# A fused attention and two-MLP kernel on one core: the last stage gets five pairs of operand buffers instead of four, and six output buffers instead of four

## The chip, the core and the metric

The kernel runs on one core of a Trainium2 chip. The metric is the device time of one launch in microseconds (us). TensorE is called PE, VectorE DVE, ScalarE ACT, GpSimd POOL; SP is the engine that here only issues transfers (its queue is "SPq" in the rows).

## What is computed

Three parts follow each other (attention, a gated MLP, a leaky MLP), all in float32:

```python
p_packed = sm_attn(p, k, v)            # softmax(p k' / 8) v, 8 batches, 8 heads, 576 x 64, 32 packs
out = sm_attn(q, p_packed, p_packed)
x = out.transpose(0, 2, 1, 3).reshape(4608, 512)
x2 = ((x @ w1) * (x @ w2)) @ w3 @ wo1          # 512 -> 1024 -> 1024 -> 512
h = x2 @ w_in                                  # 512 -> 2048
y = np.maximum(0.01 * h, h) @ w_out            # 2048 -> 512, the result
```

The change touches the last two lines, called the last stage here.

## The kernel before

**Precision.** Every operand of these products is split into a high and a low half that PE can multiply exactly enough, and each product is three matmuls (high by high, high by low, low by high). So operands come in pairs of tiles: `xh` and `xl` for x2, `gh` and `gl` for the activations.

**Last stage.** It multiplies in the manner of Strassen: seven products of sums of quarter matrices in place of eight products. The sums are called forms. The forms of x2 (seven for each group of 768 tokens, six groups) are made once, in high and low halves, by `stage`, and written to the DRAM tensor `xfd` (L557). The hidden width is cut into three parts F (3, 3 and 2 chains wide). For each F and each group, that is for 18 units `t`, `h_unit` reads the seven forms and makes h, `g_ops` makes the forms of the activations, and `o_unit` multiplies by the forms `wo` of the second weights. The product of one form of x2 takes 6 matmuls for each chain. `o_unit` adds to a running output: for F = 0 it starts it, for F = 1 and 2 `begin_o` loads the partial sums from the DRAM tensor `part` (L798), and L817 stores them to `part`, in F = 2 to `out`.

**Buffers.** `load_forms` takes a tile `xh` and a tile `xl` for each form from XF pairs of buffers and issues the two reads, 384 KB each (L660); a read can only be issued when PE has finished with the form that held the buffers before. The output tiles `o` come from OB buffers; a load at L798 into one has to wait until the store at L817 from the same buffer has landed in DRAM. All of these transfers (L557, L553, L650, L660, L687, L798, L817) stand in SP's one queue: while SP waits for one, all behind it wait too.

**Order.** The code is written unit by unit: reads of the first four forms of unit t+1, then `o_unit(t-1)` with its stores, then the reads of the other three. The order in which instructions stand on each engine is not that of the code: a scheduler lays them out by its own estimate of times, one list for each engine, and each engine works through its list in order.

**Memory.** The pool `b1` (forms of the weights `wi`, then `xr`, `xh`, `xl`, `xt`) grows from the left over what attention held; on the right the pool `wts` (converted weights `w`, and `ppT`) lies until the end of attention, and `b2` (`wo`, `gr`, `gs`, `gh`, `gl`, `o`) later takes the right side. Ahead of the last stage `make_wi(0)` builds the forms of the first weights (L535 sums, L539 casts, L135 subtractions) and `stage_b(2, 1)` makes a part of the x2 forms, both beside the last batch: its gated products `ab` (ACT copies `a` at L427, DVE multiplies at L433, ACT casts at L438, DVE subtracts at L135; PE's products at L130 go to PSUM in two tiles for each, four tiles in all) and `M` (PE at L163, ACT at L401, DVE at L135). Then PE makes x2 (L449, printed as L130) from the `ab` tiles, and after that begins the last stage at L746.

Of the kernel before, what the change touches and what calls it, by code (L numbers as in the profile page):

```python
# [55 lines left out]
def tile_kernel(ctx, tc, qT, kT, vL, pT, w12, w3b, wo1, win, wo2, out):  # L56
# [571 lines left out]
    PARTS = ((0, 3), (6, 3), (12, 2))  # L628
    TB = 3 * NB
    ORDER = (1, 2, 6, 5, 7, 4, 3)  # L630
    XF, XR, XT, GR, GS, GH, GL, OB = 4, 5, 2, 5, 2, 5, 5, 4
    wi = {m: b1.tile([P, 2, 2, 384], F32R, name=f"wi{m}") for m in ORDER}

    def form_w(w, size):
# [256 lines left out]
```

## Time and profile before

| | before |
|---|---|
| median of 3 runs | 1306.71 us (1303.98 to 1311.98) |
| the profiled execution | 1311.57 us, its span on the core 1309.8 us |
| PE matmuls busy | 1267.4 us, 97% of the span |
| PE weight loads busy | 1170.2 us, 89% |
| DVE busy | 871.9 us, 67% |
| ACT busy | 609.7 us, 47% |
| POOL busy | 102.3 us, 8% |
| chain that ended last | PE 86%, DMA 9%, DVE 2%, issue 2%, SP's queue 1% |
| mean rate of the transfers | 216 GB/s |

A busy time says how long an engine had work under way, and the chain follows from the end of the program back through whatever was waited for. The profiled execution is 4.86 us above the median and close to the slowest of the three runs.

### The profile page before, as it was taken

The page shows a single profiled execution, that of the slowest core. Times are in us where ns is not written, and L with a number is a line of the kernel's source. Part 1 is how long each engine was busy: PE and PEld are TensorE (multiplying, and loading weights), DVE is VectorE, ACT ScalarE, POOL GpSimd, SP SyncE. Part 2 cuts the span into 40 slices and gives each one's busy share as a digit, 9 for nine tenths or more (in the row PEclk, how much of TensorE's full clock was granted, in tenths as well). Part 3 has the DMA queues.
Part 4 walks back from the last instruction along what each step waited for, and adds up shares of the span by engine and source line. Part 5 has one row for each costly group of instructions (what it writes and reads, how often), then busy time and mean ns, then how long its engine had stood idle before and what let it go on. Part 6 is the DMA issues. An engine that isn't in the chain of part 4 may idle for free.

```text
span 1309.8 us, 23357 instructions
## 1 busy us (share of the span) xinstructions
PE 1267.4 (97%) x8984; PEld 1170.2 (89%) x8984; DVE 871.9 (67%) x1449; ACT 609.7 (47%) x1141; POOL 102.3 (8%) x87
## 2 busy tenths in 40 slices
PE   5999999999999999999999999989999999999898
PEld 1458998989898989899999999989999999899898
DVE  5897465776776769709865765677457549576667
ACT  3445344454545455526655546463334343443332
POOL 4543011111110100000000000000000000000000
PEclk8999999999999999999999999999999999999999
DMA  9944254666573836438789767383754583878874
GB/s 341 349 154 158 63 160 138 206 211 228 188 253 123 284 117 225 160 109 301 251 285 311 276 215 241 121 276 135 265 194 156 181 279 131 316 255 294 273 265 156
DMA packets 139375, 283.08 MB, mean 216 GB/s; under 512 B 14848, under 2 KB 66048, under 8 KB 139264
## 3 DMA queue, kind: packets, MB, share of 16 engines
q1 hardware_dynamic: 130048, 272.16, 60.9%
q10 hardware_dynamic: 9216, 9.44, 2.1%
q8 instruction: 70, 1.15, 0.4%
q14 instruction: 41, 0.34, 0.1%
HBM read 202.38 MB, written 79.17 MB: 215 GB/s over the span
## 4 chain that ended last, share of the span: by engine, by line
PE 86%; DMA 9%; DVE 2%; issue 2%; SPq 1%; ACT 0%; POOL 0%; POOLq 0%; ACTq 0%; DVEq 0%
PE mm L130 29%; PE b L746 27%; PE c L746 14%; PE a L746 7%; PE mm L379 4%; PE at L163 4%; DMA xh<-xfd 3%; DMA xl<-xfd 1%; PE at L221 1%; DMA wi<-wid 1%; DMA v<-vL 1%; DMA part<-o 1%; DMA xr<-x2d 1%; PE at L202 0%; DMA c<-w3b 0%
## 5 line engine op out<-in xcount | busy, mean ns | idle before, releaser
L130 PEld LDWEIGHTS mm<-AT,M 128*128 128x128 f32 x1536 | 208.4, 189 | 33.2 <-issue 9.7
L130 PE MATMUL mm<-AT,M 128*128 128x288 f32 x1536 | 223.9, 301 | 6.1 <-DVE M L135 2.7
L746 PE MATMUL b<-xh,wi 128*128 128x384 f32 x768 | 218.9, 337 | 9.2 <-DMA xh<-xfd 5.6
L746 PE MATMUL b<-gh,wo 128*128 128x384 f32 x768 | 213.9, 335 | 1.6 <-DVE o L709 1.4
L130 PEld LDWEIGHTS mm<-ab,W 128*128 128x128 f32 x1536 | 203.5, 188 | 8.3 <-ACT x2s L454 5.0
L130 PE MATMUL mm<-ab,W 128*128 128x288 f32 x1536 | 207.3, 295 | 0.0
L746 PEld LDWEIGHTS b<-xh,wi 128*128 128x128 f32 x768 | 141.5, 189 | 11.6 <-ACT gr L706 4.4
L746 PEld LDWEIGHTS b<-gh,wo 128*128 128x128 f32 x768 | 140.3, 188 | 2.5 <-issue 1.0
L746 PE MATMUL b<-xl,wi 128*128 128x384 f32 x384 | 129.3, 337 | 0.4 <-DMA xl<-xfd 0.4
L746 PE MATMUL b<-gl,wo 128*128 128x384 f32 x384 | 128.4, 334 | 0.0
L746 PE MATMUL c<-xh,wi 128*128 128x384 f32 x384 | 106.7, 337 | 4.1 <-DMA xh<-xfd 3.9
L746 PE MATMUL c<-gh,wo 128*128 128x384 f32 x384 | 107.2, 335 | 0.5 <-DVE o L704 0.5
L539 ACT CAST gh<-gr 128x1152 fp32r<-128x1152 f32 (+1 forms) x72 | 75.6, 1052 | 67.1 <-PE b L746 32.5
L135 DVE TENSOR_TENSOR gl<-gr,gh 128x1152 fp32r<-128x1152 f32 (+1 forms) x72 | 87.4, 1219 | 21.2 <-ACT gh L539 21.2
L433 DVE TENSOR_TENSOR ab<-mm,a 128x288 f32<-128x288 f32 x128 | 57.8, 453 | 54.4 <-PE mm L130 34.3
L539 ACT CAST gh<-gs 128x1152 fp32r<-128x1152 f32 (+1 forms) x54 | 56.9, 1054 | 61.6 <-PE b L746 32.4
L135 DVE TENSOR_TENSOR ab<-ab,ab 128x288 fp32r<-128x288 f32 x119 | 59.8, 506 | 33.7 <-ACT ab L438 32.1
L694 ACT ACTIVATE gr<-gr 128x1152 f32<-128x1152 f32 (+1 forms) x54 | 57.3, 1062 | 47.2 <-DVE gr L709 46.8
L379 PE MATMUL mm<-ab,w 128*128 128x512 f32 x128 | 61.6, 633 | 15.3 <-POOL ab L290 10.4
L438 ACT CAST ab<-ab 128x288 fp32r<-128x288 f32 x128 | 55.1, 432 | 45.3 <-DVE ab L433 45.0
L746 PEld LDWEIGHTS c<-xh,wi 128*128 128x128 f32 x384 | 69.8, 188 | 6.4 <-DMA xh<-xfd 5.6
L746 PEld LDWEIGHTS b<-xl,wi 128*128 128x128 f32 x384 | 72.5, 189 | 1.2 <-DMA xl<-xfd 1.2
(119 smaller groups left out, 2020.4 us busy)
## 6 DMA issues: line engine op xcount, KB each, us to landing
xh<-xfd SPq DMA_DIRECT2D x126, 384.0 KB, 5.6
xl<-xfd SPq DMA_DIRECT2D x126, 384.0 KB, 5.2
part<-o SPq DMA_DIRECT2D x48, 384.0 KB, 3.3
o<-part SPq DMA_DIRECT2D x48, 384.0 KB, 4.0
c<-wo SPq DMA_DIRECT2D x20, 512.0 KB, 5.1
xfd<-xt SPq DMA_DIRECT2D x49, 192.0 KB, 3.0
xfd<-xr SPq DMA_DIRECT2D x49, 192.0 KB, 3.4
raw<-kT SPq DMA_DIRECT2D x32, 288.0 KB, 5.4
```

What stands on the lines that cost most here:

```text
L130: ins = nc.tensor.matmul(dst, lhs(i), rhs(j), start=first and n == 0, stop=last and n == 2)
L135: engine.tensor_tensor(out=out, in0=x, in1=rd(hi), op=ALU.subtract)
L163: ins = nc.tensor.matmul(dst(h)[c * 32:c * 32 + 32], lhs[r, c, :], rhs(c)[r], start=True, stop=True)
L221: ins = nc.tensor.matmul(ps[r, :64], PT[:K, c, r], v[:K, c, g * 64:g * 64 + 64], start=c == 0, stop=c == 4)
L379: nc.tensor.matmul(w13p[fc], words["3", i][:, c:c + P], words["o", jc], start=w13n[fc] == 1, stop=w13n[fc] == 8)
L433: nc.vector.tensor_tensor(out=t, in0=pb[:, :TH], in1=a, op=ALU.mult)
L438: nc.scalar.copy(t[:, 0], ab32[fc, th])
L539: nc.scalar.copy(hi[step], x[step])
L694: nc.scalar.activation(out=out, in_=x, func=AF.Prelu, alpha=0.01)
L746: nc.tensor.matmul(dst, lhs(l), rhs(r), start=first and n == 0, stop=last and n == total - 1, skip_group_check=True)
```

## The change

```diff
-    XF, XR, XT, GR, GS, GH, GL, OB = 4, 5, 2, 5, 2, 5, 5, 4
+    XF, XR, XT, GR, GS, GH, GL, OB = 5, 5, 2, 5, 2, 5, 5, 6
```

XF goes from 4 to 5 pairs `xh`, `xl` and OB from 4 to 6 tiles `o`; each of the four added tiles takes 3,072 bytes of every partition. No arithmetic, no transfer and no byte is added or removed. Two things follow from it in the built program. Pool `b1` now ends at byte 86,144 of a partition instead of 79,984, and `wts` begins at 83,040, so that `b1` now reaches into the memory of `wts`: the last tiles `xt` and `xl` come to lie on `ppT` and `w`. And the scheduler lays out another order on all engines but POOL.

The first place is SP's queue at the step from F = 0 to F = 1 (`o_9927` to `o_9930` are the outputs of the last unit of F = 0, `o_10407` and on those of the next units, `wo...` the new second weights, `xh_9880`, `xh_9884` forms of the first unit of F = 1). Before:

```order
L687 DMA wo7_7437<-wod_62 128x3x256
L817 DMA part_7440<-o_9929 128x768
L798 DMA o_10409<-part_7440 128x768
L798 DMA o_10411<-part_7440 128x768
L687 DMA wo4_7438<-wod_62 128x3x256
L817 DMA part_7440<-o_9930 128x768
L660 DMA xl_9881<-xfd_81 128x768
L660 DMA xh_9880<-xfd_81 128x768
```

After:

```order
L687 DMA wo7_7437<-wod_62 128x3x256
L817 DMA part_7440<-o_9927 128x768
L798 DMA o_10411<-part_7440 128x768
L817 DMA part_7440<-o_9928 128x768
L687 DMA wo4_7438<-wod_62 128x3x256
L817 DMA part_7440<-o_9930 128x768
L817 DMA part_7440<-o_9929 128x768
L798 DMA o_10413<-part_7440 128x768
```

The load of `wo4` stood behind two loads of `o`; now it stands behind one, and ahead of it there are only a load of `o` and two stores.

The second place is SP's queue in F = 2 (`o_13339` and its like are outputs, `xh_13582` and `xh_13586` the next forms). Before:

```order
L660 DMA xh_13470<-xfd_81 128x768
L817 DMA out<-o_13339 128x768
L798 DMA o_13629<-part_7440 128x768
L660 DMA xl_13583<-xfd_81 128x768
L660 DMA xh_13582<-xfd_81 128x768
L817 DMA out<-o_13341 128x768
L817 DMA out<-o_13343 128x768
L817 DMA out<-o_13345 128x768
L798 DMA o_13631<-part_7440 128x768
L660 DMA xl_13587<-xfd_81 128x768
L660 DMA xh_13586<-xfd_81 128x768
```

After:

```order
L660 DMA xh_13470<-xfd_81 128x768
L817 DMA out<-o_13339 128x768
L660 DMA xl_13583<-xfd_81 128x768
L660 DMA xh_13582<-xfd_81 128x768
L798 DMA o_13633<-part_7440 128x768
L660 DMA xl_13587<-xfd_81 128x768
L660 DMA xh_13586<-xfd_81 128x768
L817 DMA out<-o_13343 128x768
L660 DMA xl_13591<-xfd_81 128x768
L817 DMA out<-o_13341 128x768
```

The reads of `xl_13587` and `xh_13586` stood behind three stores and a load of `o`, and now stand ahead of these three stores; the load of `o` in front of them is another one.

The third place is DVE ahead of the last stage, at the last gated products of the last batch (`ab32_7114` is the fifth of seven after `M_6921`). Before:

```order
L135 TENSOR_TENSOR M_6921<-at_6912,M_6921 128x1024
L433 TENSOR_TENSOR ab32_6952<-mm_6937,a_6950 128x288
L135 TENSOR_TENSOR xr_7201<-xr_7201,xt_7392 128x384
L433 TENSOR_TENSOR ab32_7025<-mm_7010,a_7023 128x288
L135 TENSOR_TENSOR ab_6954<-ab32_6952,ab_6954 128x288
L433 TENSOR_TENSOR ab32_7062<-mm_7047,a_7060 128x288
L135 TENSOR_TENSOR ab_7027<-ab32_7025,ab_7027 128x288
L135 TENSOR_TENSOR ab_7064<-ab32_7062,ab_7064 128x288
L433 TENSOR_TENSOR ab32_7091<-mm_7076,a_7089 128x288
L135 TENSOR_TENSOR ab_7093<-ab32_7091,ab_7093 128x288
L433 TENSOR_TENSOR ab32_7114<-mm_7099,a_7112 128x288
```

After, the rows that end with the same product:

```order
L135 TENSOR_TENSOR ab_7027<-ab32_7025,ab_7027 128x288
L433 TENSOR_TENSOR ab32_7062<-mm_7047,a_7060 128x288
L535 TENSOR_TENSOR xr_6971<-wi2_6930,xr_6963 128x384
L135 TENSOR_TENSOR wi5_6932<-xr_6961,wi5_6932 128x384
L135 TENSOR_TENSOR wi1_6929<-wi1_6929 128x384
L535 TENSOR_TENSOR xr_6987<-wi7_6933,wi4_6934 128x384
L135 TENSOR_TENSOR wi6_6931<-xr_6963,wi6_6931 128x384
L433 TENSOR_TENSOR ab32_7091<-mm_7076,a_7089 128x288
L135 TENSOR_TENSOR wi2_6930<-wi2_6930 128x384
L135 TENSOR_TENSOR wi7_6933<-xr_6965,wi7_6933 128x384
L135 TENSOR_TENSOR ab_7064<-ab32_7062,ab_7064 128x288
L433 TENSOR_TENSOR ab32_7114<-mm_7099,a_7112 128x288
```

All 22 operations of `make_wi(0)` on DVE began 53 rows ahead of `M_6921`, in front of and among the first products of the batch; now they stand behind it, among the last seven products, and the sums and subtractions of `stage_b(2, 1)` behind those. On ACT the 14 casts of `wi` moved in the same way.

## Rows read from the trace of the kernel before

**Rows 1.** PE in 50 us windows: window, length, busy (matmuls), clock, DMA share, GB/s.

```profile
750.00:800.00 50.00, 47.71 (x270) 1.00 0.74 256
...
850.00:900.00 50.00, 45.61 (x262) 1.00 0.78 265
900.00:950.00 50.00, 50.00 (x290) 1.00 0.53 185
...
1000.00:1050.00 50.00, 49.24 (x283) 1.00 0.56 182
1050.00:1100.00 50.00, 48.38 (x271) 1.00 0.61 203
1100.00:1150.00 50.00, 47.86 (x269) 1.00 0.82 295
...
1200.00:1250.00 50.00, 46.48 (x257) 0.97 0.84 289
```

**Rows 2.** What PE waited for from 560 us on: total us, times, longest.

```profile
PE b L746 <- DMA xh<-xfd: 5.6, 4, 3.2
PE c L746 <- DMA xh<-xfd: 3.9, 5, 1.7
PE b L746 <- ACT gr L706: 3.6, 2, 2.7
PE b L746 <- DVE o L709: 1.4, 2, 0.7
...
```

**Rows 3.** What SP's queue waited for from 579 us on, the same columns.

```profile
SPq L798 <- DMA part<-o: 39.7, 22, 5.1
SPq L798 <- DMA out<-o: 33.8, 15, 5.6
```

**Rows 4.** Timeline of PE, two waits: start, us, what, [idle before, its releaser].

```profile
861.74 0.44 PE L746 MATMUL b<-xh,wi 128*128 128x384 f32 x1 [2.68 <-ACT gr L706]
...
1243.10 0.66 PE L746 MATMUL b<-xh,wi 128*128 128x384 f32 x1 [3.23 <-DMA xh<-xfd]
```

**Rows 5.** Timeline of SP's queue ahead of these two waits.

```profile
848.88 5.07 SPq L798 DMA_DIRECT2D o<-part  x2
...
1235.35 0.33 SPq L798 DMA_DIRECT2D o<-part  x1
...
1236.76 0.86 SPq L660 DMA_DIRECT2D xh<-xfd  x2
```

**Rows 6.** The reads of forms, from the view of the tile xh.

```profile
DMA to landing us min/median/max: 3.0/5.6/9.0
```

**Rows 7.** Timelines of ACT (first row) and of PE through the last batch.

```profile
531.00 0.51 ACT L539 CAST xt<-xr 128x384 fp32r<-128x384 f32 x1 [4.15 <-DMA xr<-x2d]
...
532.19 1.47 PE L130 MATMUL mm<-AT,M 128*128 128x288 f32 x6 [2.64 <-ACT a L427]
533.59 1.96 PE L163 MATMUL at<-w,ppT 64*32 64x512 f32 x16
...
542.28 1.09 PE L163 MATMUL at<-w,ppT 64*32 64x512 f32 x16
...
554.67 25.47 PE L130 MATMUL mm<-ab,W 128*128 128x288 f32 x192
```

**Rows 8.** Timeline of DVE: forms of wi, then the last gated products.

```profile
518.66 1.02 DVE L135 TENSOR_TENSOR wi<-xr,wi 128x384 fp32r<-128x384 f32 x2
519.60 0.55 DVE L535 TENSOR_TENSOR xr<-wi,wi 128x384 f32<-128x384 f32 x1
...
546.88 0.45 DVE L433 TENSOR_TENSOR ab<-mm,a 128x288 f32<-128x288 f32 x1
...
548.72 0.45 DVE L135 TENSOR_TENSOR ab<-ab,ab 128x288 fp32r<-128x288 f32 x1
549.09 0.45 DVE L433 TENSOR_TENSOR ab<-mm,a 128x288 f32<-128x288 f32 x1
...
551.74 0.45 DVE L433 TENSOR_TENSOR ab<-mm,a 128x288 f32<-128x288 f32 x1
```

## The prediction, made before the changed kernel ran

> **What bounds the kernel now.** I read the windows first, then the table of what PE waits for, then SP's queue around the waits. PE is the bound: in a window of 50 us without waits the last stage runs 290 matmuls, 50/290 = 0.1724 us each [rows 1]. So only PE's gaps can be shortened. Six of the windows between 600 and 1250 us fall short; they hold 270 + 262 + 283 + 271 + 269 + 257 = 1612 matmuls where 6 x 290 = 1740 would fit, so 128 are missing, 22.1 us [rows 1]. The other seven windows hold 288 to 290, as the one at 900 us does [rows 1].
>
> The table of PE's waits says whose gaps these are. Of its eight rows the first four stand here: 5.6 + 3.9 = 9.5 us for reads of `xh`, 3.6 us for ACT's copies into `gr`, 1.4 us for DVE at the outputs at the very end of the program [rows 2]. The other four hold 0.9 us for reads of `xl`, which makes 10.4 us for reads, and 0.7 us more for DVE. That is 16.1 us. The rest of the 22.1 is PE running slowly behind a gap: in the window with the longest one the granted clock is 0.97 on average [rows 1].
>
> Why are the reads late? The queue of SP shows it. A load of `o` may go out only when the store from the same buffer has landed, and with four buffers that store is the one just issued: 39.7 + 33.8 = 73.5 us of waiting in the queue [rows 3]. Ahead of the gap at 1243 us, a load of `o` goes out only at 1235.35, when the store from its buffer has landed, the reads `xh` behind it at 1236.76, and PE stands still for 3.23 us [rows 4, 5]. The gap of 2.68 us at 861.74 is booked on ACT's copy into `gr`. But there two loads of `o` held the queue from 848.88 for 5.07 us [rows 4, 5], and `wo4`, whose cast stands ahead of that copy in ACT's list, was behind them in the order shown above. It is the same cause, one step removed.
>
> **Part 1, the pairs and the outputs in the last stage.** No work is added; reads are only issued earlier. How much, I counted in the two built orders: the matmuls between the one that releases a read (through everything ahead of it in SP's list) and the one that first uses it. Of the 252 tiles read, 24 had fewer than 40 matmuls (40 x 0.1724 = 6.9 us) before, now 6 have; below 50 (8.6 us) it was 84 and is 25. The mean goes from 93 to 125. The landings measured are 3.0 us at least, 5.6 in the median, 9.0 at most [rows 6]. So before, a read that is a little slower than the median is late at 24 places, and now at 6. For the reads of the longest gap (`xl_13587`, then `xh_13586`) the cushion grows from 43 matmuls to over 100, and they leave the place behind three stores that the second piece of the order shows. For the loads of `o` the mean cushion grows from 117 matmuls to 220.
>
> The Trainium skill, "DMA: Bandwidth & Descriptors", section "Anatomy of one DMA — SWDGE (gpsimd) path", fits a transfer as about 2.0 us plus bytes over 436,000 per us. By that an estimate for 393,216 bytes is 2.9 us, no cushion of 25 matmuls (4.3 us) would ever be too short, and the pair added would give nothing. The trace agrees with it for a read that runs alone (3.0 us) and not for the median of 5.6 us, at which several reads share the engines [rows 6].
>
> What this can give: 22.1 us less the window 1050 to 1100 (19 matmuls, 3.3 us), which holds no wait for a read of forms but the shorter of the two waits for `gr` (0.9 us) and the 0.7 us for DVE, is 18.8 us. I take three quarters, as the tight reads go from 24 to 6: **14.1 us**. The bounds are 0 (each earlier read lands later by as much, since all share the engines) and 22.1 us.
>
> **Part 2, the work ahead of the last stage.** `b1` now reaches into the memory of `wts`, and the scheduler places its first use behind the last use of that memory by PE, that is behind `M_6921`. This takes something away and adds something.
>
> Removed: PE's gap of 2.64 us at 532 us, where ACT was late with a copy `a`, because a cast of an x2 form ahead of it in ACT's list had waited 4.15 us for its data; and the slow stretch behind it, 16 matmuls in 1.96 us where the same 16 take 1.09 later [rows 7]. Together 2.64 + 0.87 = 3.5 us.
>
> Added: the 22 operations of `make_wi(0)` now stand among the last seven products on DVE. An operation on `wi` costs DVE 0.47 us (two in 519.60 - 518.66) and one on `ab` 0.37 (549.09 - 548.72) [rows 8]. From 546.88, the first of the seven products, to the fifth, `ab32_7114`, there are 7 operations of the second and 11 of the first kind: 7 x 0.37 + 11 x 0.47 = 7.8 us, so it begins at 554.6 and ends 0.45 later at 555.1; before, it began at 551.74 [rows 8]. The last of the seven products on PE needs the PSUM tile that it frees. PE has half of that product, 6 matmuls of 25.47/192 = 0.133 us [rows 7], still to do, so x2 begins at about 555.9 to 556.0 instead of 554.67 [rows 7]. That is 1.3 us. Behind it, x2's first product needs `ab_7116`, 8 rows on (3 x 0.37 + 5 x 0.47 = 3.5 us, subtracted by 558.6). The 19 matmuls ahead of that in PE's list take 2.5 us to 558.5, and 19 of the next product are put ahead of the wait, so nothing is added there. The casts on ACT lie beside this. Bounds: below, nothing is late (0); above, all of the 22 operations lie on PE's path, 22 x 0.47 = 10.3 us. I take **1.3 us**, since PSUM lets PE run two products ahead.
>
> The `wi` forms are then ready at about 563 us, and PE wants them when x2 is done, at 554.67 + 25.47 = 580 [rows 7]. That cover of 17 us hides them, and in front of it DVE has the sums of `stage_b(2, 1)` no longer. If the cover were gone, the forms would cost their own 10.3 us.
>
> **The sum.** -14.1 - 3.5 + 1.3 = -16.3 us against the profiled execution: span 1309.8 - 16.3 = 1293.5, and with the 1.8 us around it 1311.6 - 16.3 = **1295 us**. The profiled execution was 4.9 us above the median of 1306.7, so against the median the gain is 11.7 us, 0.9%. Part of what sets it above the median may be the same gaps, which is why I do not subtract the sum from the median.
>
> **The rivals.**
>
> *The wait moves on.* With the reads in time, PE meets ACT's and DVE's copies out of PSUM, or stores, at the same places. For it: 3.6 + 2.1 us of PE's waits are already booked on ACT and DVE [rows 2]. Against it: most of the former goes back to SP's queue. If half of part 1 is lost to this, 7 us, the time is 1311.6 - 7 - 2.2 = 1302 to 1303 us.
>
> *Reads were not what was short.* A read issued earlier shares the engines with more others and lands later by as much; the share in use is already 0.74 to 0.84 in the windows with gaps [rows 1]. By it only part 2 remains: 1311.6 - 2.2 = 1309 us. It is also what the fit of the Trainium skill would give. Against it: in the window around the longest gap SP was waiting for stores, not the engines for bandwidth.
>
> *Slower: landings grow past the cushions.* If the landings of all reads grew to the longest measured, 9.0 us, which is 52 matmuls [rows 1, 6], all 25 tiles with cushions under 50 would be late, some 13 pairs, by 7 matmuls or 1.2 us on average; with the slow stretch behind each gap (22.1 us missing in the six windows for 14.4 us of waits in them, a factor of 1.5) this is 23 us of loss in place of 18.8 now, so 1311.6 + 4.6 - 2.2 = 1314 us. It is slower from a landing of 8.5 us on. Against it: no byte is added, and the mean share leaves a fifth of the engines free.
>
> *Part 2 on the path.* All 10.3 us of DVE's forms count: 1295 + 9 = 1304 us.
>
> *All gaps go.* 1311.6 - 22.1 - 2.2 = 1287 us.
>
> **How the numbers follow.** The forecast, 1289 to 1300 us, has 0.55; the wait moves on 0.15; reads were not what was short 0.12; part 2 on the path 0.06; landings grow 0.05; all gaps go 0.07. The range from 1285 to 1308 us leaves out the end of the third case and most of the slower one, less than 2 in 10. About 1% is what a measurement of this kernel can tell from no change, 13.1 us: faster means below 1293.6 us, and the forecast lies just above that. Of its 0.55 some 0.34 is below, and with all gaps gone 0.41 is faster. Slower by over 1%, above 1319.8, needs the slower rival at twice its price or part 2 with no gain: 0.04. The rest, 0.55, is within 1%.
>
> **What would show it.** Right: waits of PE for `xh` and `xl` of 2 to 3 us in place of 10.4; no gap over 1 us at the step from F = 0 to F = 1; windows of 287 or more matmuls from 600 to 1250 us; waits of SP at L798 much below 73.5 us; x2 begins 1 to 2 us after the fifth product is out, with the 2.64 us gap gone. Wrong: a median landing well above 5.6 us with the same gaps; new waits of PE on ACT or DVE in the place of those on reads; a gap of 5 us or more between the last products and x2, or at the first matmul of the last stage for `wi`.

## The result, and the profile after

The changed kernel takes 1295.81 us (median of 5 runs, 1287.86 to 1297.64), and the kernel before, in 5 runs beside it, 1308.08 us. The ratio is 0.9896, with a 95% interval of 0.9856 to 0.9935: a little over 1% faster, with the bound of 1% inside the interval. The forecast was 1295 us, range 1285 to 1308. The profiled execution took 1297.09 us with a span of 1295.3, which is 14.5 us less than the span before; the forecast for it was 16.3 less.

The time is right; the terms of the sum behind it are less so. I split the span at the first matmul of the last stage (L746). Timeline of PE before (start, length, line, operation, operands):

```profile
579.98 0.34 PE L746 MATMUL b<-xh,wi 128*128 128x384 f32 x1
```

and after:

```profile
575.43 0.34 PE L746 MATMUL b<-xh,wi 128*128 128x384 f32 x1
```

The stage begins 4.55 us earlier, where part 2 of the sum had 2.2. It then lasts 1295.3 - 575.43 = 719.9 us instead of 1309.8 - 579.98 = 729.8: 9.9 us less, where part 1 had 14.1. In these two executions the errors nearly cancel. But the 4.55 is no measure to a microsecond: in the table below, four executions that have the order of before ahead of the stage begin it between 576.50 and 582.26 us, and nine that have the changed order between 575.07 and 579.27. What sets the two orders apart is seen closer by, in PE's window from 500 to 580 us (columns as in [rows 1]), before and after:

```profile
500.00:580.00 80.00, 77.36 (x601) 0.98 0.48 165
500.00:580.00 80.00, 80.00 (x625) 1.00 0.54 182
```

All nine with the changed order have 80.00 there, the four others 77.20 to 78.10: 1.9 to 2.8 us of idle time are gone.

What PE waits for in the changed kernel, the whole table from 545 us on (total us, times, longest), to be read beside [rows 2]:

```profile
PE c L746 <- DMA xh<-xfd: 3.8, 3, 1.9
PE b L746 <- DVE o L704: 2.7, 2, 2.1
PE a L746 <- DMA xh<-xfd: 1.3, 1, 1.3
PE c L746 <- DVE o L704: 0.9, 2, 0.6
PE b L746 <- DVE gl L135: 0.7, 1, 0.7
PE b L746 <- DVE o L709: 0.7, 1, 0.7
```

Reads cost 3.8 + 1.3 = 5.1 us instead of 10.4. ACT's 3.6 us for `gr` are gone. DVE has gone from 2.1 to 5.0 us. The windows of PE say where (length, busy (matmuls), clock, DMA share, GB/s), beside [rows 1]:

```profile
850.00:900.00 50.00, 48.11 (x268) 0.97 0.64 223
...
1050.00:1100.00 50.00, 46.28 (x259) 1.00 0.55 190
1100.00:1150.00 50.00, 48.67 (x280) 1.00 0.86 314
1200.00:1250.00 50.00, 48.72 (x280) 1.00 0.84 299
```

With 288 at 750 us and 290 at 1000 us, the six windows that were short now hold 288 + 268 + 290 + 259 + 280 + 280 = 1665 matmuls instead of 1612: 53 are back, 53 x 0.1724 = 9.1 us. Five of the six gained, the one at 1200 us most (23). The one from 1050 to 1100 us lost 12. The one from 850 to 900 us, at the step from F = 0 to F = 1, gained only 6 and still lacks 22. The timeline of PE has the two longest gaps that are left, one on a read in the window from 850 us, and one on DVE in the window that lost:

```profile
856.20 0.44 PE L746 MATMUL c<-xh,wi 128*128 128x384 f32 x1 [1.89 <-DMA xh<-xfd]
...
1073.24 0.44 PE L746 MATMUL b<-gh,wo 128*128 128x384 f32 x1 [2.05 <-DVE o L704]
...
```

The gap at 1073 us stands where the forms of `wi` for F = 2 are made. Timelines of SP's queue, DVE and ACT ahead of it:

```profile
1060.98 0.89 SPq L650 DMA_DIRECT2D wi<-wid  x2
...
1067.00 0.42 DVE L535 TENSOR_TENSOR xr<-wi,wi 128x256 f32<-128x256 f32 x1 [3.55 <-DMA wi<-wid]
...
1072.63 0.55 DVE L704 TENSOR_TENSOR o<-b,o 128x384 f32<-128x384 f32 x1
...
1067.00 0.73 ACT L539 CAST wi<-wi 128x256 fp32r<-128x256 f32 x2 [5.01 <-DMA wi<-wid]
```

The last loads of `wi` leave SP's queue at 1060.98. Until 1067.00 DVE (3.55 us) and ACT (5.01 us) stand idle for them, with other work queued behind. Then the sums of `wi` come first, and the sum of an output for which PE waits starts only at 1072.63.

In SP's queue the waits for loads of `o` have fallen only from 73.5 us [rows 3] to 58.4:

```profile
SPq L798 <- DMA part<-o: 38.2, 23, 4.4
...
SPq L798 <- DMA out<-o: 20.2, 11, 4.7
```

The landings of the reads are what they were, 3.1/5.7/8.7 us (least, median, most), beside [rows 6].

### The profile page after: what moved, and what is told of

Read it like the earlier page. It is cut to its first block, busy times and chain, and to the rows that moved or that the text cites. A ratio compares the mean times of both kernels' runs of the same rounds, so it can differ in the third digit from the quotient of the medians.

```text
span 1295.3 us, 23350 instructions
## 1 busy us (share of the span) xinstructions
PE 1262.9 (97%) x8984; PEld 1170.3 (90%) x8984; DVE 870.8 (67%) x1449; ACT 609.3 (47%) x1141; POOL 102.4 (8%) x87
## 4 chain that ended last, share of the span: by engine, by line
PE 87%; DMA 8%; DVE 2%; issue 1%; SPq 1%; ACT 1%; POOL 0%; ACTq 0%; DVEq 0%; POOLq 0%
PE mm L130 30%; PE b L746 28%; PE c L746 14%; PE a L746 7%; PE mm L379 4%; PE at L163 4%; DMA xh<-xfd 2%; DMA xfd<-xt 1%; DMA v<-vL 1%; PE at L221 1%; PE at L202 0%; DMA raw<-kT 0%; DMA xfd<-xr 0%; DMA wi<-wid 0%; DMA xfd<-P 0%
## 5 line engine op out<-in xcount | busy, mean ns | idle before, releaser
L130 PEld LDWEIGHTS mm<-AT,M 128*128 128x128 f32 x1536 | 207.9, 189 | 30.2 <-issue 11.7
L746 PE MATMUL b<-xh,wi 128*128 128x384 f32 x768 | 219.1, 335 | 0.0
L746 PE MATMUL b<-gh,wo 128*128 128x384 f32 x768 | 214.1, 335 | 3.4 <-DVE o L704 2.7
L746 PEld LDWEIGHTS b<-gh,wo 128*128 128x128 f32 x768 | 140.3, 188 | 4.7 <-DVE o L704 3.3
L746 PEld LDWEIGHTS b<-xh,wi 128*128 128x128 f32 x768 | 141.0, 188 | 0.3 <-ACT gr L706 0.2
L746 PE MATMUL b<-gl,wo 128*128 128x384 f32 x384 | 128.4, 334 | 0.7 <-DVE gl L135 0.7
L746 PE MATMUL b<-xl,wi 128*128 128x384 f32 x384 | 128.4, 334 | 0.0
L746 PE MATMUL c<-xh,wi 128*128 128x384 f32 x384 | 107.6, 339 | 3.8 <-DMA xh<-xfd 3.8
L746 PE MATMUL c<-gh,wo 128*128 128x384 f32 x384 | 106.9, 335 | 0.9 <-DVE o L704 0.9
L746 PEld LDWEIGHTS c<-xh,wi 128*128 128x128 f32 x384 | 70.9, 190 | 5.1 <-DMA xh<-xfd 4.2
L379 PE MATMUL mm<-ab,w 128*128 128x512 f32 x128 | 61.6, 635 | 14.1 <-POOL ab L290 9.6
L746 PEld LDWEIGHTS b<-gl,wo 128*128 128x128 f32 x384 | 72.1, 188 | 1.0 <-DVE gl L135 1.0
```

What stands on the lines that cost most here:

```text
L130: ins = nc.tensor.matmul(dst, lhs(i), rhs(j), start=first and n == 0, stop=last and n == 2)
L379: nc.tensor.matmul(w13p[fc], words["3", i][:, c:c + P], words["o", jc], start=w13n[fc] == 1, stop=w13n[fc] == 8)
L746: nc.tensor.matmul(dst, lhs(l), rhs(r), start=first and n == 0, stop=last and n == total - 1, skip_group_check=True)
```

## The experiments

Times are medians, each ratio is to the kernel before run beside it; not all rows come from one chip, so rows are compared by their ratios. "Stage" is the length of the last stage in the profiled execution, from the first matmul at L746 to the end of the span. The last two columns are PE's waits in it, in us, for reads of `xh` and `xl` and for ACT and DVE. The last four columns come from one execution each, and that of e5 was the second slowest of its twelve, that of e4 the slowest of its six.

| kernel | us | ratio, 95% interval | stage begins | stage | reads | ACT, DVE |
|---|---|---|---|---|---|---|
| before | 1308.08 | | 579.98 | 729.8 | 10.4 | 5.7 |
| after | 1295.81 | 0.9896 (0.9856 to 0.9935) | 575.43 | 719.9 | 5.1 | 5.0 |
| e1: five pairs, four outputs | 1296.34 | 0.9896 (0.9875 to 0.9917) | 577.27 | 717.6 | 4.2 | 4.9 |
| e2: four pairs, six outputs | 1309.37 | 0.9995 (0.9979 to 1.001) | 576.50 | 730.7 | 12.0 | 4.4 |
| e3: before, unused tile of 6,144 bytes | 1305.43 | 0.9971 (0.9954 to 0.9988) | 575.11 | 728.0 | 10.9 | 5.4 |
| e4: six pairs, four outputs | 1296.6 | 0.9895 (0.9873 to 0.9917) | 579.11 | 719.1 | 0 | 7.8 |
| e5: before, `o` loaded by POOL | 1313.79 | 1.0028 (1.0009 to 1.0047) | 579.78 | 736.8 | 9.4 | 10.2 |
| e6: e1, `o` loaded by POOL | 1296.22 | 0.9885 (0.9857 to 0.9913) | 575.84 | 720.4 | 2.5 | 6.8 |
| e7: e6, stores of `o` too | 1304.74 | 0.9951 (0.9928 to 0.9973) | 575.07 | 727.9 | 7.4 | 7.3 |
| e8: e1, weights loaded by POOL | 1300.91 | 0.9914 (0.9885 to 0.9943) | 576.95 | 722.4 | 1.1 | 9.7 |
| e9: after, no sums of `wi` for F = 2 | 1292.0 | 0.9861 (0.9829 to 0.9894) | 579.27 | 714.7 | 1.7 | 4.5 |
| e10: before, unused tile of 3,040 bytes | 1310.43 | 1.0008 (0.9986 to 1.003) | 582.26 | 728.2 | 9.5 | 5.1 |
| e11: after, low parts of `wi` on POOL | 1307.16 | 0.9996 (0.9979 to 1.0014) | 576.82 | 728.3 | 2.3 | 12.3 |

### The two halves apart

e1, the pairs alone:

```diff
-    XF, XR, XT, GR, GS, GH, GL, OB = 4, 5, 2, 5, 2, 5, 5, 4
+    XF, XR, XT, GR, GS, GH, GL, OB = 5, 5, 2, 5, 2, 5, 5, 4
```

> XF = 5, OB = 4. Built order: b1 reaches into wts, so the work of make_wi(0) moves behind M_6921 as in the change; reads of forms with a cushion under 40 matmuls go from 24 to 16 of 252 (the change: 6), loads of o keep their mean cushion of 118. Theory (pairs and outputs each give part of the last stage's gain): first matmul of the last stage at about 575.5 us in place of 580.0, and about half of the 10 us of the last stage: 1308 - 4.5 - 5 = 1298.5 us, ratio 0.993. Rival A (only the outputs matter, since SP's queue is held by loads of o): the first step alone, 1303.5 us, ratio 0.9965. Rival B (only the pairs matter): as the change, 1296 us, ratio 0.990.

e2, the outputs alone:

```diff
-    XF, XR, XT, GR, GS, GH, GL, OB = 4, 5, 2, 5, 2, 5, 5, 4
+    XF, XR, XT, GR, GS, GH, GL, OB = 4, 5, 2, 5, 2, 5, 5, 6
```

> XF = 4, OB = 6. Built order: make_wi(0) stays where it was; reads under 40 matmuls stay at 23, loads of o get a mean cushion of 217 matmuls in place of 117. Theory: first matmul of the last stage stays at about 580 us; the two long gaps behind waiting loads of o (2.7 us at the step from F = 0 to F = 1, 3.2 us in F = 2) go, the short ones stay: about 5 us, 1303 us, ratio 0.996, and SP's waits at the loads of o fall from 73.5 us to under 60. Rival A (outputs are what matters): 10 us, 1298 us, ratio 0.9925. Rival B (only pairs matter): 1308 us, ratio 1.000.

The outputs alone give 0.9995, nothing that can be told from no change, and 12.0 us of waits for reads. The pairs, with the work ahead of the stage that moves with them, give 0.9896, as with both. With six output buffers SP's waits for loads of `o` are what they were, 39.3 + 34.1 = 73.4 us:

```profile
SPq L798 <- DMA part<-o: 39.3, 19, 5.7
SPq L798 <- DMA out<-o: 34.1, 13, 6.4
```

And ahead of the longest gap the queue looks as in [rows 5]. SP's timeline of e2, then the gap in PE's:

```profile
1226.47 2.47 SPq L817 DMA_DIRECT2D out<-o  x3
1232.44 0.33 SPq L798 DMA_DIRECT2D o<-part  x1
...
1233.82 0.86 SPq L660 DMA_DIRECT2D xh<-xfd  x2
...
1240.12 0.66 PE L746 MATMUL b<-xh,wi 128*128 128x384 f32 x1 [3.14 <-DMA xh<-xfd]
```

The load of `o` still goes out behind three stores, 3.5 us after the last of them (1226.47 + 2.47 to 1232.44). In the built order the scheduler uses the further buffers to place these loads further ahead of their use (217 matmuls instead of 117 in the mean), and each still stands behind the store that frees its buffer. More buffers moved the load, not the wait.

### The work ahead of the stage

e3 leaves the kernel before as it is and makes `b1` larger by a tile that nothing uses, so that it reaches into the memory of `wts` as in the change (its lines are one higher, L747 for L746):

```diff
+    pad = b1.tile([P, 1536], F32, name="pad")
```

> The kernel before (XF = 4, OB = 4) with an unused tile of 6,144 bytes a partition in b1: no more buffers, but b1 ends where it does in the change and reaches into wts, so make_wi(0) moves behind M_6921. Theory: all of the part ahead of the last stage and nothing of the last stage: first matmul of the last stage at about 575.5 us in place of 580.0, PE without the gap of 2.64 us, time from there to the end as before (730 us): 1308 - 4.5 = 1303.5 us, ratio 0.9965. Rival (that the last stage began earlier comes from something else, or differs from run to run): first matmul at about 580 us, ratio 1.000; the predicted stall of 1.3 us would put it at 577 to 578.

It takes 0.9971 of the time, 3.8 us less (0.0029 x 1309; by its interval 1.6 to 6.0). In the last batch PE's timeline has no gap (the last row is cut off at the end of the window that was asked for, 560 us):

```profile
537.08 1.09 PE L163 MATMUL at<-w,ppT 64*32 64x512 f32 x16
538.10 11.62 PE L130 MATMUL mm<-AT,M 128*128 128x288 f32 x84
549.55 10.64 PE L130 MATMUL mm<-ab,W 128*128 128x288 f32 x78
```

e10 is its control, a tile so small that `b1` does not reach `wts` and the built order of every engine stays as before:

```diff
+    pad = b1.tile([P, 760], F32, name="pad")
```

> The kernel before with an unused tile of 3,040 bytes a partition instead of the 6,144 of the kernel with the larger unused tile: b1 then ends just short of the memory of wts, and the built order of every engine is the one of before, row for row. If it is the overlap with wts that gave the 0.3% there, the ratio to before is 1.000 within 0.002, and PE's gap of some 2.6 us ahead of the last batch is there. If a shift of the addresses alone does it, the ratio is 0.997.

Its ratio is 1.0008, and PE's gap is there again, with the slow stretch behind it:

```profile
534.41 1.34 PE L130 MATMUL mm<-AT,M 128*128 128x288 f32 x6 [2.20 <-ACT a L427]
535.68 1.96 PE L163 MATMUL at<-w,ppT 64*32 64x512 f32 x16
```

So the gain of this part comes from the overlap of memory and the order that follows from it, not from the size or the addresses. It comes without the pairs: 0.9971 alone, 0.9896 with them. If the two add up, which no run shows, the pairs are worth 0.0075, or 9.8 us, and by the two intervals some 3.5 us more or less.

### More of the same

e4, six pairs:

```diff
-    XF, XR, XT, GR, GS, GH, GL, OB = 4, 5, 2, 5, 2, 5, 5, 4
+    XF, XR, XT, GR, GS, GH, GL, OB = 6, 5, 2, 5, 2, 5, 5, 4
```

> XF = 6, OB = 4. Theory: the cushions of reads grow further, the loads of o still hold SP's queue: last stage some 7 us shorter, start at 575.5: 1308 - 4.5 - 7 = 1296.5 us, ratio 0.991. Rival A (outputs are what matters): as with five pairs alone, 1303.5 us, ratio 0.9965. Rival B (only pairs matter): all waits on reads go, 1308 - 4.5 - 14 = 1289.5 us, ratio 0.986.

No wait for a read is left, and the time is that of five pairs. What PE waits for instead, the first rows:

```profile
PE c L746 <- DVE o L704: 3.4, 2, 1.8
PE b L746 <- ACT o L706: 1.3, 1, 1.3
...
```

From here on the reads are not what is short.

### Is the held queue the cause at all?

e2 did not take the wait for stores out of SP's queue. e5 does, in the kernel before:

```diff
-                    nc.sync.dma_start(out=o, in_=part[F - 1, r, c0:c0 + UT].rearrange("p (j c) -> p j c", j=2))
+                    nc.gpsimd.dma_start(out=o, in_=part[F - 1, r, c0:c0 + UT].rearrange("p (j c) -> p j c", j=2))
```

> The kernel before (four pairs, four output buffers), with the 48 loads of o (L798) issued by POOL instead of SP. POOL has no other work in the last stage. Nothing that SP's queue holds now waits for a store, so the 73.5 us of waits at L798 are gone from it. Theory A (the forecast's: a held queue makes the reads late): PE's waits for xh and xl fall from 10.4 us to 2 to 4 us, the gap of 3 us near 1240 us is gone, and the time is 1300 to 1303 us. Theory B (a pair comes free too late, whatever stands in the queue): the counted matmuls between release and use hardly move (22 tiles under 40 instead of 24, mean 95 instead of 93), the waits for xh and xl stay at 8 to 11 us, and the time is 1307 to 1311 us. Against both: if a DMA issued by POOL starts much later than one by SP, PE's waits for DVE at the outputs (L704, L709) grow, and the time is above 1311 us.

For the reads theory B came out: PE's waits for them are 9.4 us, hardly less than 10.4. The time is above both theories, 0.3% slower than before, as the last case in the expectation has it: PE's waits for ACT and DVE grew from 5.7 to 10.2 us, all of the latter on DVE. Why DVE is later there stays open, so the time of e5 does not price the queue alone; the reads' waits do. What SP's queue waits for tells more. The waits of stores (first row, the largest of several) and of reads for the matmuls that free a pair, from 579 us on, in the kernel before:

```profile
SPq L817 <- DVE o L709: 135.6, 29, 17.8
SPq L660 <- PE b L746: 93.4, 53, 7.0
...
SPq L660 <- PE c L746: 33.3, 29, 4.0
SPq L660 <- PE a L746: 24.3, 11, 4.9
```

in e5:

```profile
SPq L817 <- DVE o L709: 181.6, 30, 19.1
SPq L660 <- PE b L746: 129.4, 55, 6.8
SPq L660 <- PE c L746: 52.2, 35, 4.5
SPq L660 <- PE a L746: 26.4, 17, 4.9
```

and in e1, the five pairs of above:

```profile
SPq L660 <- PE b L746: 83.5, 50, 6.2
SPq L660 <- PE c L746: 52.7, 34, 4.9
SPq L660 <- PE a L746: 24.3, 14, 5.7
```

Before, the reads waited 93.4 + 33.3 + 24.3 = 151.0 us for a free pair, and loads of `o` held the queue for 73.5. With the latter gone, the former is 208.0 us, and all waits of stores at L817 have grown from 188.8 to 234.4. The queue waits no less than before; it waits for other things. These totals do not say by themselves what is short: with five pairs (e1) the reads wait 83.5 + 52.7 + 24.3 = 160.5 us for a free pair, more than with four, and PE waits for reads 4.2 us in place of 10.4; with six pairs it is 150.1 us, and PE waits for none. What counts is the wait right ahead of a read that is late. In e5 PE has six gaps of over 0.3 us on a read of `xh`. Ahead of four of them the queue waited last for a pair (0.3 to 2.4 us), ahead of one for ACT at a store (5.7 us) and then 1.2 us for PE with a load of `wi`, and ahead of one for nothing, as many transfers of `stage` go out in a row there.

At single places the loads of `o` did decide: in the kernel before they stand ahead of the late reads at three gaps (0.76, 1.70 and 3.23 us), and the gap of 3.23 us near 1240 us is gone in e5. But a gap of 2.01 us on DVE's `gr` stands there, and one of 2.95 us on a read is new in the window of 1100 us. The timeline of PE in e5:

```profile
1129.86 0.66 PE L746 MATMUL b<-xh,wi 128*128 128x384 f32 x1 [2.95 <-DMA xh<-xfd]
```

One rival was not run: with four pairs, the stores at L817 hold SP's queue longest, and no run takes them out of it; with five pairs e7, below, does, and is slower. Also, with five pairs the scheduler puts reads ahead of stores, as the second piece of the order shows, so that an earlier free pair and a better place in the queue are not told apart.

e6 is this edit on e1. e7 is e6 with the stores (L817) on POOL's queue as well:

```diff
-            nc.sync.dma_start(out=todo[x][1], in_=todo[x][0])
+            nc.gpsimd.dma_start(out=todo[x][1], in_=todo[x][0])
```

> Five pairs, four output buffers, and the loads of o issued by POOL. With five pairs 4.2 us of PE's waits were left for reads and 4 to 5 us for DVE at the outputs. Theory A: the waits for reads go to under 1.5 us and the time to 1292 to 1294 us. Theory B: with five pairs the reads that are still late lie behind other reads or behind loads of wi, the waits stay at 3 to 5 us, and the time is 1295 to 1298 us.

> Five pairs, four output buffers, loads of o and stores of o (L798, L817) both issued by POOL, so that SP issues only reads of forms and of weights. Theory A: as with the loads alone, 1292 to 1294 us; the 159 us that SP waits at L817 are gone too, but no read stood behind them that was due, so this gives at most 1 us more. Theory B: 1295 to 1298 us. At the end of the program the last stores would leave from POOL: if that takes longer than from SP, the span grows by it.

e6 takes PE's waits for reads from 4.2 to 2.5 us, and the time is the same (0.9885 and 0.9896): DVE and ACT take it up, 6.8 us for 4.9. e7 is slower than e1, 0.9951 against 0.9896, some 7 us. Its waits for reads are back at 7.4 us, though no store of `o` stands in SP's queue any more, with one of 3.81 us at 858 us, and the longest landing of a read is 11.3 us instead of 9.2. Why the reads come later there was not followed up and stays open.

### Where part 1 lost a third

The step from F = 1 to F = 2 got worse in the changed kernel. Is it the place of the loads of `wi` in SP's queue (e8), or the work on DVE and ACT (e9)? e8 is e1 with the loads of `wi` and `wo` issued by POOL:

```diff
-                nc.sync.dma_start(out=rd(wi[m])[:, 1, a, :P * n].rearrange("p (m c) -> p m c", m=n), in_=src)
+                nc.gpsimd.dma_start(out=rd(wi[m])[:, 1, a, :P * n].rearrange("p (m c) -> p m c", m=n), in_=src)
...
-            nc.sync.dma_start(out=rd(wo[m])[:, 1, :n], in_=src)
+            nc.gpsimd.dma_start(out=rd(wo[m])[:, 1, :n], in_=src)
```

> Five pairs, four output buffers, and the loads of wi and wo (L650, L687) issued by POOL. In the changed kernel the loads of wi for F = 2 stand behind reads of forms in SP's queue from 1055 to 1061 us, DVE and ACT wait for them until 1067.0, and PE then waits 3.7 us for DVE between 1073 and 1083. If the place in SP's queue is what makes them late, they go out some 5 us earlier here, these gaps are gone, and the reads that stood behind loads of weights come earlier too (4 tiles read under 40 matmuls instead of 16): 1291 to 1293 us. If the loads are late because the last use of wi by the F = 1 products releases them late, or because DVE has too much to do there, the gaps stay and the time is 1295 to 1298 us.

The loads do not go out earlier: the last of `wi` at 1066.2 us in e8, at 1061.5 us after. POOL, which has nothing else to issue there, waits 3.58 us for the products of F = 1 before the last two. The timeline of POOL in e8:

```profile
1065.48 1.45 POOL L650 DMA_DIRECT2D wi<-wid  x2 [3.58 <-PE b L746]
```

The window from 1050 us holds 271 matmuls, not 290, and the one from 800 us only 262 (291 after), so that PE itself comes some 5 us later to this step; why it loses them at 800 us stays open. The place in SP's queue is not the cause; the loads go out when the buffer is free. By its interval the ratio of e8 is not told apart from that of e1.

e9 is the changed kernel without the work:

```diff
-            form_w({m: (wi[m][:, 0, a], wi[m][:, 1, a]) for m in ORDER}, P * n)
+            F < 2 and form_w({m: (wi[m][:, 0, a], wi[m][:, 1, a]) for m in ORDER}, P * n)
```

> The changed kernel without the sums and casts that make the forms of wi for F = 2 (their loads stay; the products of F = 2 then use forms that are partly those of F = 1, so this part of the result is not what the reference asks for). In the changed kernel these operations stand in DVE's and ACT's lists from 1067.0 us; both engines sat idle for their loads just before (3.55 and 5.01 us), and the sums of the outputs come behind them: PE waits 3.7 us for DVE from 1073 to 1083, and the window 1050 to 1100 holds 259 matmuls instead of 290. Theory: the waits at this step are what part 1 of the forecast lost; without the operations the window holds 285 or more, 26 matmuls or 4.5 us come back, and the time is 1290 to 1292 us. Rival: the step is slow for another reason (reads, weights of wo, the copies into gr), the window stays under 270 and the time at 1295 to 1297 us.

The ratio is 0.9861, and its interval (0.9829 to 0.9894) overlaps that of the changed kernel (0.9856 to 0.9935), so a gain in time is likely and not shown. The window is full. The next one is not. Windows of PE in e9:

```profile
1050.00:1100.00 50.00, 49.91 (x288) 1.00 0.66 219
1100.00:1150.00 50.00, 46.05 (x250) 0.93 0.79 273
```

The theory holds for the step itself: 288 matmuls for 259, 5.0 us. But without this work PE comes sooner to the next place, and there 3.9 us of waiting for ACT's copies into `gr`, and a granted clock of 0.93, take it all back: the two windows hold 288 + 250 = 538 matmuls, and 259 + 280 = 539 in the changed kernel. What e9 has more of lies in the windows of 850 (11 matmuls) and 1200 us (8).

e11 keeps the work and moves some of it off DVE, to POOL, which has nothing to do there (lines one higher again):

```diff
-                sub(nc.vector, lo[step], x[step], hi[step])
+                sub(eng, lo[step], x[step], hi[step])
...
-            form_w({m: (wi[m][:, 0, a], wi[m][:, 1, a]) for m in ORDER}, P * n)
+            form_w({m: (wi[m][:, 0, a], wi[m][:, 1, a]) for m in ORDER}, P * n, nc.gpsimd if F else nc.vector)
```

> The changed kernel with the low parts of the wi forms for F = 1 and F = 2 (the subtractions of L135 on wi, 14 for each F) computed by POOL, which has no other work in the last stage, instead of DVE. On DVE one costs 0.34 us when they stand in a row (1067.81 to 1069.48 for five), so some 4.7 us leave DVE's list at the step from F = 1 to F = 2, where PE waits 3.7 us for DVE between 1073 and 1083. POOL takes 0.88 us for 128x288 in an earlier stage, so some 11 us for the 14; PE wants the forms from about 1090 us on. Theory: DVE's list is what PE waits for at this step, most of the gaps go, and the time is 1291 to 1293 us. Rival: the forms come too late from POOL or ACT is behind the gaps as well: 1296 us or more.

It undoes the whole gain: 0.9996. The window from 800 us holds 251 matmuls and the one from 1050 us 252. Late forms from POOL, the rival, are not it: only 0.2 us of all waits of PE, DVE and ACT from 600 us on are for POOL. DVE became slower while POOL worked, and ACT's casts of `wi` then wait 8.4 us for DVE's sums (4.6 in the changed kernel), with the copies that PE needs behind them: PE waits 6.0 us for ACT, where it waited none. The timeline of DVE in e11, then that of POOL at the same time:

```profile
1070.25 0.42 DVE L535 TENSOR_TENSOR xr<-xr,wi 128x256 f32<-128x256 f32 x1
1070.59 0.96 DVE L535 TENSOR_TENSOR xr<-wi,wi 128x256 f32<-128x256 f32 x1
...
1072.35 0.96 DVE L535 TENSOR_TENSOR xr<-wi,wi 128x256 f32<-128x256 f32 x1
1073.23 0.55 DVE L710 TENSOR_TENSOR gr<-c,gr 128x384 f32<-128x384 f32 x1
...
1071.22 0.92 POOL L135 TENSOR_TENSOR wi<-xr,wi 128x256 fp32r<-128x256 f32 x1
```

An operation of DVE on two tiles in SBUF takes 0.42 us until POOL starts at 1070.47. Of the six of this size behind that, four take 0.94 to 0.96 us and two 0.48. One that reads PSUM (`gr<-c,gr`) takes its 0.55 us throughout.

## Why the prediction was right, and where not

**What bounds the kernel: right.** PE's gaps were what could be shortened, full windows hold 290 matmuls still, and no kernel here gained in any other way.

**Why the reads were late: the step that failed.** The forecast put it down to loads of `o` that hold SP's queue and named the one gap where that could be seen [rows 4, 5]. e2 gave them two more buffers and changed neither the 73.5 us nor the time. e5 took them out of the queue and left 9.4 of the 10.4 us. What is short is pairs: with five PE waits 4.2 us for reads (e1), with six not at all (e4), while loads of `o` still hold the queue for 59.9 and 59.2 us. How much of that is the free pair and how much the place in the queue that the scheduler gives a read is not shown. One row of SP ahead of one gap showed what stood in front of the reads there, not what would stand there next. The table of the queue's waits had larger numbers, stores (188.8 us) and free pairs (151.0), and I read from it only the two rows on `o`.

**Part 1: the mechanism half right, the size too large.** 14.1 us forecast. The stage became 9.9 us shorter, and by the timed ratios of e1 and e3 the pairs are worth 9.8 us, give or take 3.5. Two terms were wrong. The three quarters came from the count of tight reads, 24 to 6; but e1 has 16 such reads and the same time, so the count does not price the gain. And the window from 1050 to 1100 us, which I left out as unchanged, lost 12 matmuls, 2.1 us, to DVE. The window from 850 us, which I counted among those that would fill, still lacks 22, 3.8 us, with a gap of 1.89 us on a read. e9 shows that the work at the step to F = 2 costs 5.0 us in its own window, and that the next window loses as much once it is gone.

**Part 2: 2.2 us forecast, 3.8 measured (e3, 1.6 to 6.0).** By the time alone the forecast is not refuted; by the rows one of its terms is. What is removed was sized well: the gap of 2.64 us and the slow stretch [rows 7], 3.5 us together, are gone. The addition of 1.3 us did not appear. The timelines of PE (its second row cut off at 560 us) and DVE after:

```profile
538.62 11.62 PE L130 MATMUL mm<-AT,M 128*128 128x288 f32 x84
550.07 10.15 PE L130 MATMUL mm<-ab,W 128*128 128x288 f32 x75
...
540.98 0.45 DVE L433 TENSOR_TENSOR ab<-mm,a 128x288 f32<-128x288 f32 x1
...
549.53 0.46 DVE L433 TENSOR_TENSOR ab<-mm,a 128x288 f32<-128x288 f32 x1
...
556.88 0.46 DVE L135 TENSOR_TENSOR ab<-ab,ab 128x288 fp32r<-128x288 f32 x1
```

DVE's list was sized about right: from the first product behind `M_6921` (540.98) to the fifth it takes 8.55 us, where I had 7.8 and the kernel before 4.86 [rows 8]. The fifth product is read by DVE from 549.53 to 549.99, and x2 begins at 550.07, where I had expected it 0.8 to 0.9 us behind. The 84 matmuls ahead of it run on without a gap. So PE did not hold half a product back for that PSUM tile; why not was not followed further. The cover that I named is there: `wi` and `ab` are done at 557.3, and PE wants the forms at 575.43.

**The signs.** Waits for reads were to be 2 to 3 us and are 5.1. No gap over 1 us at the step from F = 0 to F = 1: wrong, the gap of 1.89 us at 856.20 us stands in the first unit of F = 1; only the gap of 2.68 us on ACT's copy [rows 4] is gone. All windows from 600 to 1250 us at 287 or more: wrong at 850, 1050, 1100, 1200 and, with 284, 1150 us. SP's waits for loads of `o` much below 73.5: 58.4, and 59.9 in e1 with four output buffers, so what they fell is not owed to the outputs. x2 1 to 2 us behind the fifth product with the gap gone: the gap is gone, the distance is 0.08 us.

**The rivals.** "The wait moves on" is true in part: with five pairs PE waits 5.0 us for DVE, where it waited 2.1, and for ACT no longer; with six all 7.8 us are on ACT and DVE (e4), and with the loads of `o` on POOL the waits on DVE grow (e5). "Reads were not what was short" falls with e1 beside e3, 0.9896 and 0.9971, whose intervals lie apart. The sentence of the Trainium skill, "DMA: Bandwidth & Descriptors", section "Anatomy of one DMA — SWDGE (gpsimd) path", from which I estimated 2.9 us for a read, would have made the pairs worth nothing; the median stayed at 5.7 us, and the pairs gave 9.8 us. That section is about transfers issued by POOL, and these reads are issued by SP, so I used its fit outside what it is for, and nothing here refutes it. Nor did the reads of 3.0 us run alone, as I wrote: three to six other transfers were under way at each of the eight quickest, five to eight at the five around the median. "Landings grow" did not happen: 8.7 us at most, 9.0 before. "All gaps go" was never near: 10.1 us of waits are left.

**The total** was right in part by luck. The sum took 16.3 us off an execution that was 4.9 us above its median; from median to median the gain is 12.3 us, close to the 11.7 that the forecast gave for this. And the pairs were in the change whatever made the reads late: with the outputs alone, by the forecast's own reason the place to begin, the gain would have been nothing (e2). No version here beats the changed kernel by more than the intervals allow; e6, at 0.9885, is level with it.

## What to carry to other kernels

Before blaming the transfer that stands at the head of a queue, ask which wait comes up next when that one is gone, and look at it for each late load by itself: the queue's total of waits stays about the same whether loads are late or not (e1, e4, e5). Here more buffers for the loads helped, and another queue for the transfers ahead of them did not. A change of buffer sizes can move work through an overlap of memory alone: run an unused tile of the same size, and one that stays short of the overlap, to price it. Once the reads are in time, look at the engine that empties PSUM: a burst of work in its list that waits for a load stands in front of everything else, and taking it away can bring up the next wait at once (e9).

## What the runs showed of the hardware

DVE's operations on two tiles in SBUF get slower while POOL works on SBUF. In e11 four of six on 128x256 take 0.94 to 0.96 us while POOL subtracts, two 0.48, where they take 0.42 without it; of those that read PSUM all 13 keep their 0.55 us. The Trainium skill, "SBUF — State Buffer", section "Who interferes with whom", says that a DVE instruction with two SBUF inputs contends with a GpSimd instruction that reads SBUF, and that one with at most one SBUF input, outside certain modes that use two ports, does not; the rows agree with both. So moving 28 operations (14 for each of F = 1 and F = 2) off a crowded DVE to an idle POOL cost about 1% (0.9996 against 0.9896) instead of giving 3 to 5 us.

Whether a DMA issued by POOL lands as fast as one issued by SP is not settled here: its median was 1.4 us longer for one kind of load and 0.8 us shorter for another. For loads of `o` it took 3.4/5.4/7.6 us (least, median, most) in e5 and 3.2/4.0/8.2 on SP before, for the 16 loads of `wi` in the last stage 3.6/4.7/6.6 us in e8 and 2.4/5.5/7.2 on SP in the changed kernel. The issue itself is longer on POOL: 0.746 us in the median for these loads of `wi`, 0.424 on SP.
